# A decode layer bound by its loads: V in 32 KB runs over four large slots, P turned by selection products, wo in one transfer

## The chip, the cores and the metric

One core of a Trainium2 chip. The metric is the device time of one execution in microseconds. The kernel before takes 214.79 us (median of 3 runs, 214.47 to 214.87). Faster or slower needs 2%, here 4.3 us; each step is timed in five rounds against the kernel before on the same chip.

## The reference, cut to what matters

```python
x = layernorm(A_x)                                 # 4 batches, 1 token, D = 576
q = (x @ wq)                                       # 32 heads of 128
k, v = k_cache[:, :, -2048:], v_cache[:, :, -2048:]  # 16 heads, each for two q heads; 33.5 MB each
p = softmax(q k^T * 128**-0.5)
attn = (p v) @ wo                                  # wo: 4096 x 576, 4.7 MB
h  = gelu(layernorm(x) @ w1); x1 = x + shifted(h) @ w2
mlp  = x1 + gelu(layernorm(x1) @ w3) @ w4          # w3, w4: 5.3 MB each
out = A_x + attn + mlp
```

Everything is bf16 and almost everything is read once: 88.5 MB for four tokens.

## The kernel before

A single queue of transfers runs from the first microsecond to the last: weights, 16 chunks of K, 16 chunks of V with half of wo between them, the other half of wo, w4 in five pieces. The MLP is computed at the start, only its product with w4 waits for the end. The parts that the change touches:

```python
# four slots of 2 MB for K and then for V; chunk c is 4 heads of one batch, 16 KB runs
def kv_pairs(cache, c):
    b, gq = CH[c]
    return [(ring_t[:, (c % NPOS) * UE:(c % NPOS + 1) * UE],
             cache[b, NU * gq:NU * gq + NU, Sk - W:Sk, :].rearrange("g (i t) d -> i g (t d)", t=NT))]
...
for c in range(NC):
    add_dma(kv_pairs(A_v_cache, c), ("v", c % NPOS), [f"PV{c - NPOS}" if c >= NPOS else t_done(c + NC - NPOS)], KS + c)
# wo in two halves: one behind the fourth V chunk, one behind the last (WO_AT = (3.5, 15.5))
ev_wo = [add_dma([(wo_v[:, 16 * h:16 * h + 16, :], wo_s[:, 16 * h:16 * h + 16, :])], ("wo", h), ["h2_3"], KS + WO_AT[h]) for h in range(2)]
...
# P turned: transpose on DVE, one product with a permutation, copy on ACT
add("dve", lambda e, q=q: e.transpose(out=PTx[:, q, :], in_=P_sb[:, q, :]), waits=[f"exp{q}"], ...)
...
# product with V: 64 matmuls of N = 8 a chunk
ins = e.matmul(o_, lhsT=slot_t(c)[:, t, :], rhs=PTpad[:, c % 2, t].rearrange("p u e -> p (u e)"), ...)
...
# product with wo: 32 matmuls for each half, each half waiting for its own transfer
for h in range(2):
    add("pe", pe_AO(h), waits=["ORT", ev_wo[h]], sig=f"AO{h}", key=KT - 1 + 0.1 * h)
...
IDLE = ((3, -2.7), (7, 0.5), (5, 20.5))   # matmuls on zeros near the end, to hold PE's clock up
```

## Time and profile before

| | kernel before |
|---|---|
| time, span of the profiled run | 214.79 us, 213.3 us |
| read | 88.5 MB, 415 GB/s over the span |
| transfer engines in the V stage | full, 428 GB/s |
| PE in the V stage | 11.09 us busy of 30, at half clock |
| last links of the chain | w4's transfer, then 1.4 us of PE and a copy |

PE is the matmul engine (TensorE), DVE is VectorE, ACT is ScalarE, Pool is GpSimd; DMA stands for the 16 transfer engines. A "run" of V, K or wo is one piece of memory without a gap, moved by one transfer record; "clock" is the share of its full clock that PE was granted.

The views are read from the whole to the part: the page's forty slices tell which engine is full when, the chain tells what ended last, the windows give a stage's busy times, and the timeline gives durations and, in square brackets, how long an engine stood idle before an entry and for whom. The lines are shown in the prediction.

### The profile page before, as it was taken

Reading aid. Unit: us, or ns where it says so; the run is one execution under the profiler, and the core shown is the slowest. Engines: PE = TensorE matmul, PEld = TensorE weight load, DVE = VectorE, ACT = ScalarE, POOL = GpSimd, SP = SyncE. Lnnn points to the kernel's source line nnn. Section 1 sums busy time; section 2 is a strip of 40 time slices with the busy share of each in tenths; the row PEclk is TensorE's granted clock in tenths of the full one; section 3 lists DMA queues with packets and bytes.
Section 4 is the critical chain, followed back from the end, with each engine's and each line's share of the span. In section 5 each row is a group of like instructions: output and inputs, shape, how many; then the busy total and the mean of one; then the engine's idle time right before and its main releaser. Section 6 shows DMA issues by size and latency. Waiting matters only on the chain. (4 is left out here: it accounts for less than half of the span.)

```text
span 213.3 us, 5930 instructions
## 1 busy us (share of the span) xinstructions
PE 143.1 (67%) x2679; PEld 110.1 (52%) x2679; DVE 75.3 (35%) x148; ACT 61.6 (29%) x76; POOL 10.9 (5%) x38
## 2 busy tenths in 40 slices
PE   0048469999999999999996377133434433336995
PEld 0023246887788878888774067133434433334542
DVE  0242700767666666666664830100010001001000
ACT  2001204566556666666656620000000000000000
POOL 8300000000010000000000000000000000000000
PEclk9999959999999999999999555555555555555799
DMA  7999999999999999999999999999999999999993
GB/s 289 413 389 480 422 406 427 424 429 424 430 427 427 433 427 427 426 430 430 424 433 427 421 440 417 421 433 427 424 424 433 427 424 433 430 426 437 426 405 131
DMA packets 6446, 88.65 MB, mean 416 GB/s; under 512 B 744, under 2 KB 884, under 8 KB 1444
## 3 DMA queue, kind: packets, MB, share of 16 engines
q1 hardware_dynamic: 6420, 88.50, 97.8%
q8 instruction: 8, 0.13, 0.2%
q14 instruction: 2, 0.02, 0.0%
q10 hardware_dynamic: 16, 0.01, 0.0%
HBM read 88.49 MB, written 0.00 MB: 415 GB/s over the span
## 5 line engine op out<-in xcount | busy, mean ns | idle before, releaser
L343 PE MATMUL ps<-perm_bf,ring 128*128 128x128 bf16 x1024 | 62.1, 219 | 0.9
L343 PEld LDWEIGHTS ps<-perm_bf,ring 128*128 128x128 bf16 x1024 | 57.5, 98 | 9.6 <-issue 9.4
L350 DVE COPY kt<-ps 128x1024 bf16<-128x1024 bf16 x80 | 52.3, 687 | 26.1 <-PE ps L343 25.9
L349 ACT ACTIVATE kt<-ps 128x1024 bf16<-128x1024 bf16 x48 | 48.9, 1025 | 30.1 <-PE ps L343 28.9
L424 PE MATMUL ps<-PTpad,ring 128*128 128x8 bf16 x1024 | 29.7, 168 | 41.3 <-PEq L586 37.6
L424 PEld LDWEIGHTS ps<-PTpad,ring 128*128 128x128 bf16 x1024 | 28.7, 104 | 42.5 <-issue 42.4
L563 ACT ACTIVATE out_sb<-ps 4x288 bf16<-4x288 f32 x1 | 0.4, 403 | 87.4 <-PE ps L441 87.4
L357 PE MATMUL ps<-kt,Qs 128*32 128x512 bf16 x272 | 17.8, 382 | 1.4 <-PEq L586 1.4
L413 DVE TENSOR_TENSOR PTpad<-PT,mU_bf 128x512 bf16<-128x512 bf16 x16 | 6.4, 422 | 30.1 <-PE ps L424 30.1
L436 DVE TENSOR_TENSOR OTn<-ps,rinvB 128x32 bf16<-128x32 f32 x4 | 0.8, 192 | 33.9 <-PE ps L424 33.9
L279 PE MATMUL ps<-ident_bf,xn_bf 4*128 4x4 bf16 x8 | 0.6, 170 | 13.7 <-DVE ragsrc L273 13.7
L357 PEld LDWEIGHTS ps<-kt,Qs 128*32 128x32 bf16 x272 | 5.7, 95 | 6.8 <-issue 1.5
L378 POOL COPY Qs<-Qpad 128x128 bf16<-128x128 bf16 x16 | 4.6, 296 | 86.4 <-PE ps L357 72.4
L279 PEld LDWEIGHTS ps<-ident_bf,xn_bf 4*128 4x128 bf16 x8 | 0.4, 112 | 13.7 <-issue 11.3
L525 PE MATMUL ps<-w,x1nT 128*32 128x387 bf16 (+7 forms) x90 | 6.0, 411 | 2.1 <-DMA w<-in_B_w_dram 1.8
L525 PEld LDWEIGHTS ps<-w,x1nT 128*32 128x32 bf16 x90 | 4.6, 126 | 3.4 <-DMA w<-in_B_w_dram 2.1
L441 PE MATMUL ps<-w,ORT 128*4 128x288 bf16 x64 | 5.5, 344 | 0.4 <-DVE ORT L463 0.4
L562 DVE CAST out_sb<-ps 4x288 bf16<-4x288 f32 x1 | 0.4, 445 | 14.5 <-PE ps L441 14.5
L441 PE MATMUL ps<-w,h2T_sb 128*4 128x288 bf16 x72 | 5.0, 286 | 0.6 <-DMA w<-in_B_w_dram 0.6
L395 PE MATMUL ps<-kt,permT_bf 128*128 128x512 bf16 x4 | 2.4, 608 | 4.3 <-DVE kt L394 4.1
L263 ACT ACTIVATE sd<-mv 4x1 f32<-4x1 f32 x3 | 0.6, 203 | 14.5 <-DVE mv L261 14.5
L441 PEld LDWEIGHTS ps<-w,ORT 128*4 128x4 bf16 x64 | 3.2, 102 | 2.9 <-DVE ORT L463 1.0
(102 smaller groups left out, 65.7 us busy)
## 6 DMA issues: line engine op xcount, KB each, us to landing
ring<-in_A_k_cache_dram SPq DMA_DIRECT2D x16, 2048.0 KB, 14.4
ring<-in_A_v_cache_dram SPq DMA_DIRECT2D x16, 2048.0 KB, 17.4
w<-in_B_w_dram SPq DMA_DIRECT2D x1, 4608.0 KB, 24.1
w<-in_A_wo_dram SPq DMA_DIRECT2D x2, 2304.0 KB, 21.0
kt<-in_A_wq_dram SPq DMA_DIRECT2D x1, 4096.0 KB, 13.2
w<-in_B_w_dram SPq DMA_DIRECT2D x1, 2592.0 KB, 28.0
w<-in_B_w_dram SPq DMA_DIRECT2D x3, 576.0 KB, 14.2
w<-in_B_w_dram SPq DMA_DIRECT2D x1, 1296.0 KB, 30.6
```

Of the source, the lines that this page charges most:

```text
L279: e.transpose(XTps[idx][:, r, :], v[:, r, :], ident_bf[0:B, 0:B])
L343: ins = e.transpose(tb[n % 4][:, t, :], slot_t(c)[:, 8 * k + t, :], perm_bf[:])
L349: return "act", lambda e: e.activation(out=ktbuf[:, n % 16], in_=tb[n % 4], func=ACTF.Copy)
L350: return "dve", lambda e: e.tensor_copy(out=ktbuf[:, n % 16], in_=tb[n % 4])
L357: ins = e.matmul(Sps[32 * u:32 * u + 32, q, :].rearrange("p (t i) -> p t i", t=16), lhsT=Qs[:, c % NPOS, 32 * u:32 * u + 32], rhs=ktgrp[:, ...
L378: P(lambda e, c=c, cc=cc: e.tensor_copy(out=Qs[:, c % NPOS, :], in_=Qpad_t[:, 128 * cc:128 * cc + 128]), waits=["qT", "qs_zero"] + ([f"SC{ ...
L395: add("pe", lambda e, q=q: e.matmul(ps[:, 4 + q % 3, :], lhsT=permT_bf[:], rhs=PTx[:, q, :], start=True, stop=True), waits=[f"PTx{q}", "pe ...
L413: return lambda e: e.tensor_tensor(out=PTpad[:, c % 2], in0=PTv[:, :, cc, :].unsqueeze(2).to_broadcast([128, NT, NU, 2]), in1=mU_bf[:].uns ...
L424: ins = e.matmul(o_, lhsT=slot_t(c)[:, t, :], rhs=PTpad[:, c % 2, t].rearrange("p u e -> p (u e)"), start=(t == 0), stop=(t == NT - 1))
L436: add("dve", lambda e, hv=hv: e.tensor_tensor(out=hv(OTn), in0=OTps.rearrange("p (b h) -> p b h", b=B), in1=hv(rinvB), op=ALU.mult), waits ...
L441: return e.matmul(ACC[h], lhsT=lhsT, rhs=rhs, start=start, stop=stop, tile_position=(0, 32 * h), skip_group_check=True)
L525: ins = e.matmul(H2ps[k][32 * g:32 * g + 32, :].rearrange("p (x c) -> p x c", c=9)[:, :, off:off + cnt], lhsT=x_, rhs=w[:, base_:base_ + 1 ...
```

## The change

The intent is to carry V in half as many runs of twice the length. A transfer is now 4 MB: the 32 heads of two batches, a quarter of the keys, so each partition gets a run of 32 KB. Four slots of 4 MB are found in the rooms of w4, w3 and the ring. Since heads now lie across the partitions, P has to be turned otherwise: the exponentials are written with a stride, and 16 products with 0/1 selection matrices bring the right rows together. The product with V has N = 64 instead of 8, its operand is made by DVE in quarters ("pads"). wo moves into a V slot, so it can only come behind V, and comes whole.

```diff
-WO_AT = (3.5, 15.5)
-HOPS = (("K", 15), ("V", 2))
+HOPS = (("K", 15), ("V", 5))
...
+        vslot = [w4_t[:, 0:VE], w3_t[:, 0:VE], ring_t[:, 0:VE], ring_t[:, VE:2 * VE]]
+        P_exp = P_sb.rearrange("p (i q t) -> p q t i", i=NI, q=4)
...
-        for c in range(NC):
-            add_dma(kv_pairs(A_v_cache, c), ("v", c % NPOS), [f"PV{c - NPOS}" if c >= NPOS else t_done(c + NC - NPOS)], KS + c)
-        ev_wo = [add_dma([(wo_v[:, 16 * h:16 * h + 16, :], wo_s[:, 16 * h:16 * h + 16, :])], ("wo", h), ["h2_3"], KS + WO_AT[h]) for h in range(2)]
+        for c in range(8):
+            b, q = c // 4, c % 4
+            add_dma([(vslot[q], v_heads[32 * b:32 * b + 32, Sk - W + 4 * VT * q:Sk - W + 4 * VT * (q + 1), :].rearrange("h (i t) d -> h i (t d)", i=4))],
+                    ("v", q), [f"PV{c - 4}_3"] if b else v_free[q], KS + c)
+        ev_wo = add_dma([(w4_t[:, 0:32 * D], A_wo.rearrange("(p r) n -> p (r n)", r=32))], "wo", ["PV4_3"], KS + 8)
...
-            add("dve", lambda e, q=q: e.transpose(out=PTx[:, q, :], in_=P_sb[:, q, :]), waits=[f"exp{q}"], sig=f"PTx{q}", key=k0)
+                for i in range(4):
+                    ins = e.matmul(ps[:, 4 + g, :].rearrange("p (q t) -> p q t", q=4), lhsT=sel[:, g // 2, g % 2, i, :], rhs=P_v[:, i],
+                                   start=(i == 0), stop=(i == 3))
...
-                    ins = e.matmul(o_, lhsT=slot_t(c)[:, t, :], rhs=PTpad[:, c % 2, t].rearrange("p u e -> p (u e)"),
+                for t in range(VQ):
+                    ins = e.matmul(OTps, lhsT=vt[:, VQ * j + t, :], rhs=pads[:, j, t].rearrange("p h e -> p (h e)"),
...
-        for h in range(2):
-            add("pe", pe_AO(h), waits=["ORT", ev_wo[h]], sig=f"AO{h}", key=KT - 1 + 0.1 * h)
+        add("pe", pe_AO, waits=["ORT", ev_wo], sig="AO", key=KT - 1)
```

More of the change, by code (lines that the diff above doesn't have):

```diff
@@ L70, in bass_parallel_sum__sliding_block_cached__mixer_s_mlp__decode_kernel @@
         w4_t = sb("w4", [128, 36 * D], BF16)
-        PTpad_t = sb("PTpad", [128, 2 * NT * 2 * NU], BF16)
+        sel_t = sb("sel", [128, 16 * 128], BF16)
         PT_t = sb("PT", [128, NT * 32], BF16)
@@ L75, in bass_parallel_sum__sliding_block_cached__mixer_s_mlp__decode_kernel @@
         ktgrp = kt_t[:].rearrange("p (s t u i) -> p s t u i", s=8, t=16, u=NU)
-        P_sb = kt_t[:, 0:2048].rearrange("p (q x) -> p q x", q=4)
-        PTx = kt_t[:, 2048:4096].rearrange("p (q x) -> p q x", q=4)
-        PTpad = PTpad_t[:].rearrange("p (s t u e) -> p s t u e", s=2, t=NT, u=NU)
-        PTv = PT_t[:].rearrange("p (t c e) -> p t c e", t=NT, c=NC)
+        VT = W // 16
+        VE = VT * Dh
+        VQ = VT // 4
+        vslot = [w4_t[:, 0:VE], w3_t[:, 0:VE], ring_t[:, 0:VE], ring_t[:, VE:2 * VE]]
+        P_sb = kt_t[:, 0:W]
+        P_exp = P_sb.rearrange("p (i q t) -> p q t i", i=NI, q=4)
+        P_v = P_sb.rearrange("p (q i t) -> p i q t", q=4, i=4)
+        pads = kt_t[:, 2 * W:2 * W + 4 * VQ * 64].rearrange("p (j t h e) -> p j t h e", j=4, t=VQ, e=2)
+        PTv = PT_t[:].rearrange("p (b q t e) -> p b q t e", b=2, q=4, e=2)
+        sel = sel_t[:].rearrange("p (b e i x) -> p b e i x", b=2, e=2, i=4)
         wqmain = kt_t[:].rearrange("p (r n) -> p r n", r=4)
-        q_sb = PTpad_t[:, 0:1024]
+        q_sb = sel_t[:, 0:1024]
         h2g = PT_t[:, 0:1152]
-        wo_v = w3_t[:, 0:32 * D].rearrange("p (r n) -> p r n", r=32)
+        wo_v = w4_t[:, 0:32 * D].rearrange("p (r n) -> p r n", r=32)
         w3r = [w3_t[:, r * F:(r + 1) * F] for r in range(4)]
@@ L116, in bass_parallel_sum__sliding_block_cached__mixer_s_mlp__decode_kernel @@
         ones_f = sb("ones_f", [128, 128], FP32)
-        mU = sb("mU", [128, NU], FP32)
-        mU_bf = sb("mU_bf", [128, NU, 2], BF16)
+        mU = sb("mU", [128, 32], FP32)
+        mU_bf = sb("mU_bf", [128, 32, 2], BF16)
         diag = sb("diag", [128, 128], FP32)
@@ L138, in bass_parallel_sum__sliding_block_cached__mixer_s_mlp__decode_kernel @@
         rinvps = ps[:, 3, 0:128]
-        OTps = ps[:, 6, 0:32]
+        OTps = ps[:, 2, 256:320]
         Qps = [ps[:, 4 + k, :] for k in range(2)]
@@ L208, in bass_parallel_sum__sliding_block_cached__mixer_s_mlp__decode_kernel @@
         P(lambda e: e.memset(ones_f[:], 1.0), sig="ones_f", key=-89)
-        add("dve", lambda e: e.tensor_reduce(out=mU[:], in_=ident_f[:].rearrange("p (i u) -> p u i", u=NU), axis=AX.X, op=ALU.add),
+        add("dve", lambda e: e.tensor_reduce(out=mU[:], in_=ident_f[:].rearrange("p (h i) -> p h i", i=4), axis=AX.X, op=ALU.add),
             waits=["ident_f"], sig="mU", key=-8)
+        P(lambda e: e.memset(sel_t[:], 0.0), waits=["qTp"], sig="sel_zero", key=3.5)
+        ident_s = ident_bf[:].rearrange("p (u b x e) -> p b e x u", u=NU, b=2, x=8)
+        for n in range(16):
+            b, e_, i = n // 8, n // 4 % 2, n % 4
+            P(lambda e, b=b, e_=e_, i=i: e.tensor_copy(out=sel[:, b, e_, i, :].rearrange("p (x u k) -> p x u k", u=NU, k=4)[..., i], in_=ident_s[:, b, e_]),
+              waits=["sel_zero", "ident_bf"], sig=f"sel{n}", key=3.51 + 0.01 * n)
         for x in range(2):
@@ L233, in bass_parallel_sum__sliding_block_cached__mixer_s_mlp__decode_kernel @@
             add_dma(kv_pairs(A_k_cache, c), ("k", c % NPOS), [t_done(c - NPOS)] if c >= NPOS else [], c)
-        for c in range(NC):
-            add_dma(kv_pairs(A_v_cache, c), ("v", c % NPOS), [f"PV{c - NPOS}" if c >= NPOS else t_done(c + NC - NPOS)], KS + c)
-        wo_s = A_wo.rearrange("(p r) n -> p r n", r=32)
-        ev_wo = [add_dma([(wo_v[:, 16 * h:16 * h + 16, :], wo_s[:, 16 * h:16 * h + 16, :])], ("wo", h), ["h2_3"], KS + WO_AT[h]) for h in range(2)]
+        v_heads = A_v_cache.rearrange("b h s d -> (b h) s d")
+        v_free = [["hT1", "hs1", "h2_3"], ["h2_3"], [t_done(NC - 3)], [t_done(NC - 1)]]
+        for c in range(8):
[3 more added lines that the diff above has]
+        ev_wo = add_dma([(w4_t[:, 0:32 * D], A_wo.rearrange("(p r) n -> p (r n)", r=32))], "wo", ["PV4_3"], KS + 8)
         w4tile, w4cols, ev_w4, W4N = [], [], [], []
@@ L240, in bass_parallel_sum__sliding_block_cached__mixer_s_mlp__decode_kernel @@
         for n, rc in enumerate(W4_ROWS):
-            v = w4_t[:, len(w4tile) * D:(len(w4tile) + rc) * D]
+            t0 = len(w4tile)
+            v = w3_t[:, t0 * D:(t0 + rc) * D] if n < 2 else ring_t[:, (t0 - 27) * D:(t0 - 27 + rc) * D]
             ev_w4.append(add_dma([(v, B_w4[base:base + 128 * rc, :].rearrange("(p r) n -> p (r n)", r=rc))], ("w4", n),
-                                 ["hT1", "hs1", "h2_3"] if n == 0 else [], KT + 5 + n))
-            W4N.append((len(w4tile), len(w4tile) + rc))
+                                 ["PV5_3" if n < 2 else "PV6_3"], KT + 5 + n))
+            W4N.append((t0, t0 + rc))
             for r in range(rc):
@@ L387, in bass_parallel_sum__sliding_block_cached__mixer_s_mlp__decode_kernel, with pe_PT, f @@
         for q in range(4):
-            add("act", lambda e, q=q: e.activation(out=P_sb[:, q, :], in_=Sps[:, q, :], func=ACTF.Exp,
+            add("act", lambda e, q=q: e.activation(out=P_exp[:, q], in_=Sps[:, q, :].rearrange("p (t i) -> p t i", t=16), func=ACTF.Exp,
                                                    bias=negb[:, 0:1], scale=scale, accum_out=rs4[:, q:q + 1]),
                 waits=["negb"], sig=f"exp{q}", key=KS + 0.1 + 0.01 * q)
-        for q in range(4):
-            k0 = KS + 0.2 + 0.1 * q
-            add("dve", lambda e, q=q: e.transpose(out=PTx[:, q, :], in_=P_sb[:, q, :]), waits=[f"exp{q}"], sig=f"PTx{q}", key=k0)
-            add("pe", lambda e, q=q: e.matmul(ps[:, 4 + q % 3, :], lhsT=permT_bf[:], rhs=PTx[:, q, :], start=True, stop=True),
-                waits=[f"PTx{q}", "permT_bf"] + (["PT0"] if q == 3 else []), sig=f"PTy{q}", key=k0)
-            add("act", lambda e, q=q: e.activation(out=PT_t[:, 512 * q:512 * (q + 1)], in_=ps[:, 4 + q % 3, :], func=ACTF.Copy),
-                waits=[f"PTy{q}"], sig=f"PT{q}", key=k0 + 0.16)
+        def pe_PT(g):
+            def f(e):
+                ins = None
+                for i in range(4):
+                    ins = e.matmul(ps[:, 4 + g, :].rearrange("p (q t) -> p q t", q=4), lhsT=sel[:, g // 2, g % 2, i, :], rhs=P_v[:, i],
+                                   start=(i == 0), stop=(i == 3))
+                return ins
+            return f
+        for g in range(4):
+            add("pe", pe_PT(g), waits=[f"exp{q}" for q in range(4)] + ["sel15"], sig=f"PTy{g}", key=KS + 0.2 + 0.1 * g)
+            pt_o = PTv[:, g // 2, :, :, g % 2]
+            pt_i = ps[:, 4 + g, :].rearrange("p (q t) -> p q t", q=4)
+            if g % 2 == 0:
+                add("act", lambda e, o=pt_o, i=pt_i: e.activation(out=o, in_=i, func=ACTF.Copy), waits=[f"PTy{g}"], sig=f"PT{g}", key=KS + 0.3 + 0.1 * g)
+            else:
+                add("dve", lambda e, o=pt_o, i=pt_i: e.tensor_copy(out=o, in_=i), waits=[f"PTy{g}"], sig=f"PT{g}", key=KS + 0.9 + 2 * (g // 2))
         add("dve", lambda e: e.tensor_reduce(out=rsum[:], in_=rs4[:], axis=AX.X, op=ALU.add), waits=["exp3"], sig="rsum", key=KS + 0.8)
@@ L403, in bass_parallel_sum__sliding_block_cached__mixer_s_mlp__decode_kernel @@
         add("pe", lambda e: e.matmul(rinvps, lhsT=ones_f[:], rhs=diag[:], start=True, stop=True), waits=["diag", "ones_f", "exp3"],
-            sig="rinvp", key=KS + 0.9)
+            sig="rinvp", key=KS + 0.55)
         add("dve", lambda e: e.tensor_copy(out=rinvB[:].rearrange("p (c u e) -> p c u e", u=NU, e=2),
                                            in_=rinvps.rearrange("p (u c e) -> p c u e", u=NU, e=2)),
-            waits=["rinvp"], sig="rinvB", key=KS + 1.5)
-        def dve_pad(c):
-            b, gq = CH[c]
-            cc = 4 * b + gq
-            return lambda e: e.tensor_tensor(out=PTpad[:, c % 2],
-                                             in0=PTv[:, :, cc, :].unsqueeze(2).to_broadcast([128, NT, NU, 2]),
-                                             in1=mU_bf[:].unsqueeze(1).to_broadcast([128, NT, NU, 2]), op=ALU.mult)
@@ L417, in pe_PV, with dve_pad @@
-        def pe_PV(c):
-            b, gq = CH[c]
-            o_ = OTps[:, 8 * b:8 * b + 8]
+            waits=["rinvp"], sig="rinvB", key=KS + 2)
+        def dve_pad(c, j):
+            b, q = c // 4, c % 4
+            return lambda e: e.tensor_tensor(out=pads[:, j],
+                                             in0=PTv[:, b, q, VQ * j:VQ * (j + 1), :].unsqueeze(2).to_broadcast([128, VQ, 32, 2]),
+                                             in1=mU_bf[:].unsqueeze(1).to_broadcast([128, VQ, 32, 2]), op=ALU.mult)
@@ L421, in f, with pe_PV @@
+        def pe_PV(c, j):
+            q = c % 4
+            vt = vslot[q].rearrange("p (t d) -> p t d", t=VT)
             def f(e):
                 ins = None
-                for t in range(NT):
-                    ins = e.matmul(o_, lhsT=slot_t(c)[:, t, :], rhs=PTpad[:, c % 2, t].rearrange("p u e -> p (u e)"),
-                                   start=(t == 0), stop=(t == NT - 1))
-                return ins
-            return f
-        for c in range(NC):
-            w = [f"PV{c - 2}"] if c >= 2 else [f"PT{q}" for q in range(4)] + ["mU_bf1"]
-            b, gq = CH[c]
-            add("dve", dve_pad(c), waits=w, inc=[(tok("pad"), 1)], key=KV + 2 * max(c - 1, 0) + 0.2)
-            add("pe", pe_PV(c), waits=[take("pad"), take(("v", c % NPOS), 16)] + ([take("otn")] if b == 0 else []), sig=f"PV{c}",
-                key=KV + 2 * c, loop=("V", gq))
-            if b == B - 1:
-                hv = lambda t, gq=gq: t[:, 0:128].rearrange("p (b h) -> p b h", b=B)[:, :, 8 * gq:8 * gq + 8]
-                add("dve", lambda e, hv=hv: e.tensor_tensor(out=hv(OTn), in0=OTps.rearrange("p (b h) -> p b h", b=B), in1=hv(rinvB), op=ALU.mult),
-                    waits=["rinvB", f"PV{c}"], sig=f"OTn{gq}" if gq == 3 else None, inc=[(tok("otn"), 1)] if gq < 3 else [], key=KV + 2 * c + 0.1)
@@ new lines, in f @@
+                for t in range(VQ):
+                    ins = e.matmul(OTps, lhsT=vt[:, VQ * j + t, :], rhs=pads[:, j, t].rearrange("p h e -> p (h e)"),
+                                   start=(q == 0 and j == 0 and t == 0), stop=(q == 3 and j == 3 and t == VQ - 1))
+                return ins
+            return f
+        for c in range(8):
+            b, q = c // 4, c % 4
+            for j in range(4):
+                add("dve", dve_pad(c, j), waits=[f"PV{c - 1}_{j}"] if c else [f"PT{g}" for g in ((0, 1) if j == 0 else (2, 3))] + ["mU_bf1"],
+                    inc=[(tok("pad"), 1)], key=KV + 2 * c + 0.2 * j)
+                add("pe", pe_PV(c, j), waits=[take("pad")] + ([take(("v", q), 16)] if j == 0 else []) + ([take("otn")] if j == 0 and q == 0 else []),
+                    sig=f"PV{c}_{j}", key=KV + 2 * c + 0.2 * j, loop=("V", b))
+            if q == 3:
+                cols = slice(64 * b, 64 * b + 64)
+                add("dve", lambda e, cols=cols: e.tensor_tensor(out=OTn[:, cols], in0=OTps, in1=rinvB[:, cols], op=ALU.mult),
+                    waits=["rinvB", f"PV{c}_3"], sig="OTn1" if b else None, inc=[] if b else [(tok("otn"), 1)], key=KV + 2 * c + 2.5)
@@ L449, in pe_idle, with pe_AO @@
             return f
-        def pe_AO(half):
-            def f(e):
-                ins = None
-                for r in range(16 * half, 16 * half + 16):
-                    for h in range(2):
-                        ins = acc_mm(e, h, ORT[:, :, r], wo_v[:, r, HALF * h:HALF * (h + 1)], start=(r == 0))
-                return ins
-            return f
+        def pe_AO(e):
+            ins = None
+            for r in range(32):
+                for h in range(2):
+                    ins = acc_mm(e, h, ORT[:, :, r], wo_v[:, r, HALF * h:HALF * (h + 1)], start=(r == 0))
+            return ins
         KH = -58.0
-        add("dve", lambda e: e.transpose(out=OTy[:].rearrange("p b r -> p (b r)"), in_=OTn[:]), waits=["OTn3"], sig="OTy", key=KT - 3)
+        add("dve", lambda e: e.transpose(out=OTy[:].rearrange("p b r -> p (b r)"), in_=OTn[:]), waits=["OTn1"], sig="OTy", key=KT - 3)
         add("pe", lambda e: e.matmul(ORps, lhsT=permT_bf[:], rhs=OTy[:].rearrange("p b r -> p (b r)"), start=True, stop=True),
@@ L463, in bass_parallel_sum__sliding_block_cached__mixer_s_mlp__decode_kernel @@
         add("dve", lambda e: e.tensor_copy(out=ORT[:].rearrange("p b r -> p (b r)"), in_=ORps), waits=["ORp"], sig="ORT", key=KT - 2)
-        for h in range(2):
-            add("pe", pe_AO(h), waits=["ORT", ev_wo[h]], sig=f"AO{h}", key=KT - 1 + 0.1 * h)
+        add("pe", pe_AO, waits=["ORT", ev_wo], sig="AO", key=KT - 1)
         def pe_t1(e):
```

## The prediction

> **What bounds the kernel now.** I read the page's slices first, because they tell which engine is full at every moment, then the chain that ended last, then the windows by stage, then the order of time in the V stage and at the end. The three lines of the page on transfers:
>
> ```profile
> DMA  7999999999999999999999999999999999999993
> GB/s 289 413 389 480 422 406 427 424 429 424 430 427 427 433 427 427 426 430 430 424 433 427 421 440 417 421 433 427 424 424 433 427 424 433 430 426 437 426 405 131
> DMA packets 6446, 88.65 MB, mean 416 GB/s; under 512 B 744, under 2 KB 884, under 8 KB 1444
> ```
>
> The transfer engines are full in every slice but the first and the last, at about 427 GB/s, whatever the compute engines do. The kernel reads 88.65 MB and the change reads the same bytes. The windows by stage (length, then busy time of each engine, then clock, DMA share, GB/s) say the same for K and for V:
>
> ```profile
> 45.00:105.00 60.00, 59.22 (x991) 48.66 (x989) 40.52 (x62) 38.13 (x38) 3.26 (x11) 1.00 1.01 428
> 142.00:172.00 30.00, 11.09 (x384) 10.74 (x384) 2.14 (x6) 0.00 (x0) 0.00 (x0) 0.50 1.01 428
> ```
>
> In the V stage PE works 11.09 of 30 us, and at half clock; DVE works 2.14. What V waits for is the landing of V. The chain in order of time ends so:
>
> ```profile
> 177.79 32.21 DMA w<-in_B_w_dram
> 210.00 0.04 issue
> 210.04 1.40 PE ps L441 x18
> 211.44 0.43 DVE out_sb L562
> ```
>
> The last link is the queue of transfers itself; PE adds a tail of some 1.4 us and one copy. So a change is worth what it takes off the transfers' total, unless it empties the queue on the way or lengthens what PE has to do after the last landings. The timeline around the last V chunks shows the pitch of a transfer:
>
> ```profile
> 183.54 1.85 PE L424 MATMUL ps<-PTpad,ring 128*128 128x8 bf16 x64 [2.90 <-PEq L586]
> 188.43 1.85 PE L424 MATMUL ps<-PTpad,ring 128*128 128x8 bf16 x64 [3.04 <-PEq L586]
> 193.32 1.85 PE L424 MATMUL ps<-PTpad,ring 128*128 128x8 bf16 x64 [3.04 <-PEq L586]
> ```
>
> One 2 MB chunk (128 runs of 16 KB) each 4.89 us. With 128 runs over 16 engines each engine carries 8 runs, so 611 ns a run; the single transfer records of the trace have a median of 613 ns for a 16 KB run.
>
> **What the Trainium skill says.** (1) "DMA: Bandwidth & Descriptors", section "Why small descriptors are slow (HBM only)": a fixed cost per packet and per descriptor comes on top of the bytes; its section on 436 GB/s puts a ceiling of 435.2 GB/s on the ports. The trace agrees in kind: the records' medians are 613 ns for 16 KB, 688 for 18 KB, 773 for 20.25 KB, 1213 for 32 KB (wq) and 1364 for 36 KB (w3). From 16 to 32 KB the slope is 600 ns for 16 KB more, so 13 ns of each run are fixed: 427.6 GB/s at 16 KB and 432 at 32 KB. (2) Same page, "Latency and other measured facts", the row on HBM row pitch at large powers of two: copies with a row pitch of 512 KiB ran at 207 GB/s per direction, 2 MiB at 164, 4 MiB at 103, a padded pitch at 214. (3) Same page, "The descriptor swizzle": each engine writes four neighbouring partitions of each half. Before, four neighbouring partitions are the same 16 KB piece of four heads, so the engines read 16 KB apart inside one head; after, they are the four 32 KB pieces of one head, so the engines read one head (8192 keys x 128 x 2 B = 2 MiB) apart. The page's pitch of 512 KiB puts its engines also four rows, 2 MiB, apart, and lost 3% (207 against 214). No run here shows yet what this does to loads. (4) "TensorE: Matmul & The Clock Gate", "Wait — 56ns, not 53.3ns?": back to back, a matmul takes N / 1.2 GHz at half clock and never less than about 25 ns. The trace has 64 matmuls of N=8 in 1.85 us, 29 ns each, which agrees with a floor.
>
> **The change part by part.**
> V's runs. Before: 16 chunks x 8 runs per engine = 128 runs x 613 ns = 78.46 us. After: 8 x 8 = 64 runs x 1213 ns = 77.63 us. Gain 0.83 us, on the path that sets the end.
> wo whole. Before 2 x 8 runs of 18 KB x 688 ns = 11.01 us; after 8 runs of 36 KB x 1364 ns = 10.91. Gain 0.10 us, on the path. w4 keeps its five pieces. Sum of the queue: -0.93 us.
> Product with V. Still 1024 matmuls, but N goes from 8 to 64. At half clock that is an estimate of 64/1.2 = 53 ns, so 128 x 53 = 6.8 us for each 4 MB chunk; at full clock the 29 ns floor gives 3.7. A chunk lands every 8 x 1213 ns = 9.7 us, so it stays hidden.
> Pads on DVE. Before 422 ns for 512 columns, 16 times. After 2048 columns, 32 times: at most 4 x 422 = 1.69 us, 6.8 us per chunk. They wait only for the preceding product on the same quarter, so they are made while V is still in flight: hidden.
> The turn of P. Removed: four DVE transposes (2.7 us) and four products. Added: 16 selection products of N=512, at half clock 512/1.2 = 427 ns each, 6.8 us, after all four exponentials. Before, exp ended at 121.95 and the first product started at 125.29; after, I put it at 122 + 6.8 + 0.8 (last copy) + 1.7 (pad) = about 131. The first chunk's slot is free at about 138.
> Does the queue run dry? The last V landing before is at 193.3 with 16 x 4.89 + 5.5 (half of wo) behind K, so K ended near 109.6. Four slots of 9.7 us reach to 148.4; the fifth transfer needs the first slot, free at 138: 10 us to spare. Later each slot frees some 7 us after its landing with 29 us queued. wo needs chunk 4 used, w4 chunks 5 and 6: each is issued before the transfer ahead of it is through. Never dry.
> The selection matrices: one clearing (Pool's Qpad clearing of 2080 columns took 1.82 us) and 16 small copies, early in the K stage, when Pool has over 70 us of idle: nothing.
> The end on PE. Before, half of wo was there at 196.97 and the first half of that product ran early. After, whole wo lands where its second half did, 193.3 + 5.5 - 0.93 = 197.9. The 64 matmuls took 5.48 us, partly at half clock; w4's products took 36 in 2.37 us, 66 ns each, so 4.2 to 5.5 us. With the small product 0.65, warming 1.69, w4's parts 2.37 + 1.25 + 1.27 and the last 18 in 1.3, PE ends between 210.5 (limited by the transfers) and 211.9, against 211.4 before. So between nothing and 1.4 us of the queue's gain can be taken back here; I charge 0.25.
> Total: 214.79 - 0.93 + 0.25 = 214.1 us.
>
> **The rivals.**
> A. The transfers slow down because the 16 engines read at 2 MiB multiples in step. For: the skill's row; the transfers before are laid out so that engines are 16 KB apart. Against: at that spacing the page lost only 3%, and within each engine 128 KB are read in one piece. 3% of 77.63 is 2.4 us: 216.5. If the loss were that of the 2 MiB row (164 of 214), V would take 101 us and the kernel 238.
> B. The tail: PE, not the last transfer, sets the end, since no part of wo's product can run early. It makes 214.3 to 215.2.
> C. PE or DVE becomes the bound of the V stage. For: at half clock PE is busy 6.8 of 9.7 us, and DVE up to 6.8. Against: both have about 30% to spare, a PE that busy might be granted its full clock, and four slots absorb jitter. If both ran in series, 13.6 us per chunk, it would add some 31 us; the quarters, each with its own pad, are there to prevent that.
> D. Nothing: run length does not matter, and 613 against half of 1213 is noise of different places in the kernel: 214.8.
>
> **Range and chances.** The plain sum is -0.4%. A gain over 2% would need 4.3 us, but at the ports' ceiling of 435.2 all 88.65 MB would take 203.7 us and V itself could win only 78.46 - 77.1 = 1.4 us; so 1%. A loss over 2% needs 4.3 us more, that is A worse than the comparable row of the skill, or C: 11%. The rest, 88%, is within 2%. Predicted 214.1 us; range 213.3 to 217.0, the upper side long because of A.
>
> **What would show it.** Right: GB/s of some 431 in the V slices, landings of V about 9.7 us apart, DMA at 9 in all slices, still a chain that ends in w4's transfer. Product with V of about 53 ns per matmul at half clock, or 29 at full. Wrong by A: V slices under 420 GB/s with the DMA share still 1.00. Wrong by B: a chain whose last 10 us are PE, with wo's product starting near 198 and no wait for w4's last piece. Wrong by C: DMA tenths under 9 in the V stage and the queue waiting for PE's products just before it issues.

## The result, and the profile after

The changed kernel takes 216.43 us (median of 6 runs, 215.72 to 217.06), the kernel before 214.59 in the same rounds. The ratio is 1.0082 (95% interval 1.0057 to 1.0107). A ratio is the mean time of one kernel's runs over that of the other's of the same rounds, so not quite the ratio of the medians quoted. Executions over 1.5% slower than the fastest of the same kernel are left out of the means. So the kernel is 0.8% slower: within 2%, and inside the predicted range, but on the other side of zero from the predicted 214.1. Note also the scatter: 1.3 us from run to run where the kernel before has 0.4. The profiled run is the slowest of the six (217.06, span 215.7).

The slices of the changed kernel (clock of PE in tenths, share of the transfer engines, GB/s):

```profile
PEclk9999969999999999999999556999799967888599
DMA  7999999999999999999999999999999999999970
GB/s 292 402 404 462 437 407 425 422 427 422 428 434 425 422 434 425 433 428 425 441 431 444 431 437 428 425 434 422 437 416 444 413 456 413 447 410 429 405 317 5
```

The queue never runs dry in the V stage, as predicted, but it is over before the span is: the last slice has 5 GB/s where the kernel before had 131. The window of the V stage, in the changed kernel:

```profile
142.00:172.00 30.00, 21.11 (x629) 20.31 (x625) 24.60 (x23) 0.00 (x0) 0.00 (x0) 0.94 1.01 431
```

V moves at 431 GB/s instead of 428. PE and DVE are far busier than before (21.11 and 24.60 of 30 us against 11.09 and 2.14) and still have room. The chain that ended last, in order of time:

```profile
165.09 34.05 DMA w<-in_A_wo_dram
199.13 0.14 issue
199.27 7.16 PE ps L465 x68
206.43 0.16 issue
206.59 1.46 PE ps L471 x6
208.04 2.30 PE ps L465 x36
210.34 1.18 PE ps L471 x5
211.53 2.35 PE ps L465 x36
213.87 0.43 DVE out_sb L583
```

It ends no longer with w4's transfer but with wo's, and behind it stand 14.6 us of PE without a wait for data: the products with wo and w4 (L465) and the matmuls on zeros (L471). The timelines of PE's end, first the kernel before:

```profile
196.97 5.48 PE L441 MATMUL ps<-w,ORT 128*4 128x288 bf16 x64 [0.38 <-DVE ORT L463]
202.37 0.65 PE L441 MATMUL ps<-t,ident_f 4*4 4x288 f32 x4
202.96 1.69 PE L447 MATMUL ps<-zeros_bf 128*128 128x512 bf16 x7
204.91 2.37 PE L441 MATMUL ps<-w,h2T_sb 128*4 128x288 bf16 x36 [0.26 <-DMA w<-in_B_w_dram]
```

and the changed kernel:

```profile
193.15 0.23 PE L483 MATMUL ps<-OTy,permT_bf 128*128 128x128 bf16 x1
199.27 6.58 PE L465 MATMUL ps<-w,ORT 128*4 128x288 bf16 x64 [5.89 <-DMA w<-in_A_wo_dram]
205.78 0.65 PE L465 MATMUL ps<-t,ident_f 4*4 4x288 f32 x4
207.97 2.37 PE L465 MATMUL ps<-w,h2T_sb 128*4 128x288 bf16 x36
```

Before, the product with wo began at 196.97, when its operand was ready. After, PE stands still for 5.89 us until wo has landed at 199.27 and then needs 6.58 us for the same 64 matmuls. Before, PE had to wait 0.26 us for w4 at 204.91; after, w4's pieces lie ready at 207.97. So two things are to be explained: why PE's end grew, and why wo landed at 199.27 when the sum had it at 197.9.

Inside the turn of P one term was far from its estimate without harm. The exponentials, before and after:

```profile
L388 ACT ACTIVATE kt<-ps,negb 128x512 bf16<-128x512 f32 x4 | 2.7, 686 | 2.6 <-DVE negb L385 2.6
```

```profile
L403 ACT ACTIVATE kt<-ps,negb 128x512 bf16<-128x512 f32 x4 | 9.4, 2702 | 2.6 <-DVE negb L400 2.6
```

Written with a stride of 64 elements, the same 512 results take 2702 ns instead of 686. The first product with V starts at 137.2 instead of the estimated 131. The slots cover it: the next transfer of V was issued at 141.3, about 7 us before the queue would have been empty (estimated at 148.4 in the prediction).

**The theories.** T, "tail": PE's work behind the landing of wo sets the end, and it is long because the clock falls to half while PE waits. Its rivals: R, "transfers": the last landing itself is later, PE only happens to end there; W, "work": the 64 matmuls need 6.6 us at any clock; and for what remains, F, "fetch": PE's instruction fetches, which run on the same transfer engines, hold up one of them.

### The profile page after: what moved, and what is told of

Same layout as the page of the kernel before. It is cut to its first block, busy times and chain, and to the rows that moved or that the text cites. A ratio compares the mean times of both kernels' runs of the same rounds, so it can differ in the third digit from the quotient of the medians.

```text
span 215.7 us, 5968 instructions
## 1 busy us (share of the span) xinstructions
PE 153.5 (71%) x2688; PEld 118.5 (55%) x2691; DVE 104.4 (48%) x160; ACT 67.9 (31%) x74; POOL 15.5 (7%) x55
## 5 line engine op out<-in xcount | busy, mean ns | idle before, releaser
L364 ACT ACTIVATE kt<-ps 128x1024 bf16<-128x1024 bf16 x48 | 49.1, 1024 | 31.1 <-PE ps L358 29.8
L436 DVE TENSOR_TENSOR kt<-PT,mU_bf 128x2048 bf16<-128x2048 bf16 x32 | 37.1, 1217 | 10.3 <-PE ps L447 10.1
L447 PE MATMUL ps<-kt,ring 128*128 128x64 bf16 x512 | 20.2, 211 | 14.5 <-PEq L607 10.2
L447 PEld LDWEIGHTS ps<-kt,ring 128*128 128x128 bf16 x512 | 19.7, 110 | 14.9 <-issue 14.9
L447 PE MATMUL ps<-kt,w 128*128 128x64 bf16 x512 | 16.3, 193 | 7.0 <-PEq L607 5.8
L447 PEld LDWEIGHTS ps<-kt,w 128*128 128x128 bf16 x512 | 15.5, 98 | 7.8 <-issue 7.4
L411 PE MATMUL ps<-kt,sel 128*128 128x512 bf16 x16 | 5.5, 516 | 12.2 <-ACT kt L403 12.2
L465 PE MATMUL ps<-w,ORT 128*4 128x288 bf16 x64 | 6.6, 392 | 5.9 <-DMA w<-in_A_wo_dram 5.9
L411 PEld LDWEIGHTS ps<-kt,sel 128*128 128x128 bf16 x16 | 1.9, 124 | 15.8 <-ACT kt L403 12.7
L403 ACT ACTIVATE kt<-ps,negb 128x512 bf16<-128x512 f32 x4 | 9.4, 2702 | 2.6 <-DVE negb L400 2.6
L465 PEld LDWEIGHTS ps<-w,ORT 128*4 128x4 bf16 x64 | 3.9, 115 | 8.4 <-issue 6.0
```

What stands on the lines that cost most here:

```text
L364: return "act", lambda e: e.activation(out=ktbuf[:, n % 16], in_=tb[n % 4], func=ACTF.Copy)
L403: add("act", lambda e, q=q: e.activation(out=P_exp[:, q], in_=Sps[:, q, :].rearrange("p (t i) -> p t i", t=16), func=ACTF.Exp, bias=negb[: ...
L411: ins = e.matmul(ps[:, 4 + g, :].rearrange("p (q t) -> p q t", q=4), lhsT=sel[:, g // 2, g % 2, i, :], rhs=P_v[:, i], start=(i == 0), stop ...
L436: return lambda e: e.tensor_tensor(out=pads[:, j], in0=PTv[:, b, q, VQ * j:VQ * (j + 1), :].unsqueeze(2).to_broadcast([128, VQ, 32, 2]), i ...
L447: ins = e.matmul(OTps, lhsT=vt[:, VQ * j + t, :], rhs=pads[:, j, t].rearrange("p h e -> p (h e)"), start=(q == 0 and j == 0 and t == 0), s ...
L465: return e.matmul(ACC[h], lhsT=lhsT, rhs=rhs, start=start, stop=stop, tile_position=(0, 32 * h), skip_group_check=True)
```

## The experiments

Unless said otherwise a run has five rounds. Times are medians.

**e1: wo in halves again, behind V.**

```diff
-        ev_wo = add_dma([(w4_t[:, 0:32 * D], A_wo....)], "wo", ["PV4_3"], KS + 8)
+        ev_wo = [add_dma([(w4_t[:, 16 * h * D:16 * (h + 1) * D], wo_s[:, 16 * h * D:16 * (h + 1) * D])], ("wo", h), ["PV4_3"], KS + 8 + 0.1 * h)
+                 for h in range(2)]
-        add("pe", pe_AO, waits=["ORT", ev_wo], sig="AO", key=KT - 1)
+        for h in range(2):
+            add("pe", pe_AO(h), waits=["ORT", ev_wo[h]], sig=f"AO{h}", key=KT - 1 + 0.1 * h)
```

> The changed kernel, but wo comes in two transfers of 2.36 MB again, one behind the other after V, and its 64 products with wo in two groups of 32, each waiting for its own half. Theory 'tail' (PE's work behind the landing of wo sets the end): the first 32 products run before wo's second half lands, PE has some 3 us less to do behind it, PE waits for the last piece of w4 again, and the time falls from 216.4 to about 215 (limited by the last landing, which in the changed kernel's profile was some 0.6 us later than before). Rival 'transfers' (the last landing sets the end): no change, or 0.1 us more for the shorter runs: 216.4.

Measured: 215.33 us (215.0 to 216.92), ratio 1.0045 (1.0018 to 1.0071). PE's timeline:

```profile
193.65 2.13 PE L467 MATMUL ps<-w,ORT 128*4 128x288 bf16 x32 [0.38 <-DVE ORT L489]
199.34 3.15 PE L467 MATMUL ps<-w,ORT 128*4 128x288 bf16 x32 [3.57 <-DMA w<-in_A_wo_dram]
```

The first half now runs at 193.65 and 1.1 us of the loss is gone; R alone is out. But in this profile the second half, still behind an idle stretch, takes 3.15 us where the first took 2.13, and the rest of PE's end was again without waits. Half the work moved, the clock not cured.

**e2: PE kept busy until wo lands.**

```diff
-IDLE = ((3, -2.7), (7, 0.5), (5, 20.5))
+IDLE = ((3, -2.7), (20, -1.5), (7, 0.5), (5, 20.5))
```

> The changed kernel, but 20 matmuls on zeros are put on PE between the turn of the output and the product with wo, so that PE has no idle stretch before wo lands. Theory 'clock' (the 64 products with wo ran 6.58 us because the clock had fallen to half in the 5.9 us in which PE waited): they take 4.2 us now, and the time falls by up to 2.4 us, to about 214.5 to 215.2, with less scatter from run to run. Rival 'work' (the 64 products take 6.6 us whatever the clock): time unchanged at 216.4 or later by up to 0.5. Rival 'transfers': unchanged.

Measured: 215.19 us (215.03 to 215.21), ratio 1.0028 (1.0015 to 1.0041), against 216.43 for the changed kernel. PE's timeline:

```profile
194.00 4.48 PE L471 MATMUL ps<-zeros_bf 128*128 128x512 bf16 x20
199.20 4.09 PE L465 MATMUL ps<-w,ORT 128*4 128x288 bf16 x64 [0.72 <-DMA w<-in_A_wo_dram]
```

Twenty matmuls on zeros fill the gap, and the same 64 products take 4.09 us instead of 6.58, with wo landing at the same moment. That refutes W. The clock in the same stretches, the changed kernel and then e2:

```profile
197.00:199.00 2.00, 0.00 (x0) 0.00 (x0) 0.00 (x0) 0.00 (x0) 0.00 (x0) 0.64 0.97 415
199.00:201.00 2.00, 1.73 (x16) 1.05 (x18) 0.00 (x0) 0.00 (x0) 0.00 (x0) 0.50 1.02 435
```

```profile
197.00:199.00 2.00, 1.48 (x7) 0.49 (x5) 0.00 (x0) 0.00 (x0) 0.00 (x0) 1.00 1.02 435
199.00:201.00 2.00, 1.80 (x30) 1.48 (x32) 0.00 (x0) 0.00 (x0) 0.00 (x0) 1.00 0.99 425
```

So the clock did fall inside the gap, and did not where the gap was filled. The scatter falls from 1.3 us to 0.2, so nearly all of it came with PE's end. The chain ends with w4's transfer again. T is shown, and its size: 216.43 - 215.19 = 1.24 us.

**b1: the kernel before, with wo alone moved.**

```diff
-        ev_wo = [add_dma([(wo_v[:, 16 * h:16 * h + 16, :], ...)], ("wo", h), ["h2_3"], KS + WO_AT[h]) for h in range(2)]
+        ev_wo = add_dma([(w3_t[:, 0:32 * D], A_wo.rearrange("(p r) n -> p (r n)", r=32))], "wo", ["h2_3"], KS + 15.5)
```

(and the 64 products in one group, as in the change)

> The kernel before with one part of the change alone: wo in one transfer behind all of V, and its 64 products in one group. Theory 'tail': nothing is gained or lost in the bytes, but PE waits for wo at half clock and has all 64 products to do behind its landing (198.8): time 216 to 217, with PE at the end of the chain and no wait for w4's last piece. Rival (the tail is peculiar to the new V stage): unchanged at 214.5.

Measured: 218.29 us (217.63 to 219.05), ratio 1.0183 (1.0167 to 1.0199): more than expected, 3.8 us for this one part. PE's timeline:

```profile
200.83 5.53 PE L441 MATMUL ps<-w,ORT 128*4 128x288 bf16 x64 [7.66 <-DMA w<-in_A_wo_dram]
```

Here PE waits 7.66 us, and from wo's landing to the last copy it works 13.6 us without a wait for data (14.6 in the changed kernel). So the tail does not belong to the new V stage, it belongs to wo coming late and whole. But b1 is no clean test of its size, because the edit did a second thing. The half of wo that stood between the fourth and the fifth V chunk had kept the queue filled while P was turned; without it the queue runs short, as the window shows (the kernel before, then b1):

```profile
125.00:130.00 5.00, 3.48 (x125) 3.45 (x126) 0.61 (x2) 0.00 (x0) 0.00 (x0) 0.50 1.02 428
125.00:130.00 5.00, 4.53 (x161) 4.48 (x162) 1.15 (x3) 0.00 (x0) 0.00 (x0) 0.50 0.71 265
```

By the transfer records, counted as below from the mean end of w3, the last piece of w4 lands 2.1 us later than in the kernel before. The profiled run of b1 is 3.0 us over that of the kernel before, so about 0.9 us are left for PE's tail (an estimate from one profile each).

**e3: V in 16 KB runs, all else as changed.**

```diff
-            add_dma([(vslot[q], v_heads[...].rearrange("h (i t) d -> h i (t d)", i=4))],
+            add_dma([(vslot[q][:, VE // 2 * x:VE // 2 * (x + 1)], v_src[:, :, VE // 2 * x:VE // 2 * (x + 1)]) for x in range(2)],
-                ... [take(("v", q), 16)] ...
+                ... [take(("v", q), 32)] ...
```

> The changed kernel with V in runs of 16 KB: each 4 MB chunk is two transfers of 2 MB (each takes half of every 32 KB run), all else as it is. By the sum of the prediction V costs 128 x 613 against 64 x 1213 ns for each transfer engine, 0.83 us more: the landing of the last V chunk and of wo come 0.8 us later and the time goes to about 217.2, with V slices of 428 instead of 432 GB/s. Rival (run length does nothing, 432 is an accident of the place): unchanged at 216.4 and 432 GB/s.

Measured: 217.5 us (216.29 to 218.18), ratio 1.0138 (1.0110 to 1.0166). About 1.1 us more than the changed kernel, in the expected direction; but with PE's tail at the end the scatter is as large as the effect. The window of the V stage has 426 GB/s. Hence:

**e5: the same on top of e2**, where the last landing sets the end.

> The kernel e2_pe_warm (PE kept busy ahead of wo, so that the last landing sets the end: 215.19) with V in runs of 16 KB as in e3. Only the run length differs from e2, and the tail of PE no longer adds its scatter. By the prediction's term (128 x 613 against 64 x 1213 ns): 0.83 us more, 216.0. Rival (the longer runs gain nothing at the last landing, since the slowest transfer engine sets it): 215.2.

Measured: 215.94 us (215.45 to 216.12), ratio 1.0059 (1.0045 to 1.0073), so 0.75 us more than e2 with its 32 KB runs. The windows of the V stage, e2 and then e5:

```profile
142.00:172.00 30.00, 23.08 (x680) 22.58 (x677) 24.75 (x24) 0.00 (x0) 0.00 (x0) 0.89 1.01 430
```

```profile
142.00:172.00 30.00, 22.52 (x690) 21.94 (x686) 25.04 (x24) 0.00 (x0) 0.00 (x0) 0.94 1.01 425
```

The term for the run length, 0.83 us, is right within the scatter. So the change does gain what it was made for. Yet e2, which has this gain and no tail, is still 0.6 us behind the kernel before (ratio 1.0028). About 1.4 us are lost elsewhere at the last landing.

**Where the rest goes: the slowest of 16 engines.** A transfer has landed when all 16 transfer engines have done their eight runs, so the landing is that of the latest engine, while GB/s is their mean. The single transfer records make this visible: at each change of size (V to wo, wo to w4) the first record of the new size is found for each of the 16 engines. The records carry no number of their engine; each is put behind the record that ends where it begins, and such a reconstruction is good to some 0.06 us. The result, in us; "lag" is how far the latest engine is behind the mean of the 16, in the one profiled run, while the time is the median of all runs:

| kernel | instruction fetches in all | lag at the end of V | lag at the end of wo | time |
|---|---|---|---|---|
| before | 8 | 0.97 | 0.97 | 214.5 |
| b1 | 8 | 1.35 | 1.36 | 218.29 |
| changed | 10 | 0.72 | 1.97 | 216.43 |
| e1 | 10 | 0.75 | 1.95 | 215.33 |
| e2 | 10 | 1.41 | 1.76 | 215.19 |
| e3 | 10 | 0.71 | 1.91 | 217.5 |
| e5 | 10 | 0.78 | 1.94 | 215.94 |
| e4 (below) | 14 | 1.75 | 1.62 | 217.06 |

Counted from the mean end of w3, where both kernels still do the same, the mean engine reaches w4's first piece after 169.67 us before and after 169.17 us in the changed kernel: 0.50 us earlier. The latest engine reaches it after 170.64 and 171.14: 0.50 us later. The gain is there on average and gone at the latest engine, which in the changed kernel falls back by 1.25 us while wo is moving. At that moment, about 1 us before the mean engine is through with wo, the records show one 16 KB fetch of instructions, 1.10 us long, and the run of wo that begins where it ends took 1.83 us instead of 1.36. The other fetches of the changed kernel's V stage look alike: 1.06 to 1.10 us, and behind each a run of V about 0.5 us longer than the median of 1.216. Fetch and longer run together take about 1.55 us of one engine. Followed from record to record, the engine with the fetch in wo is the latest one at w4's first piece, in the changed kernel and also in e1, e2, e3, e5, e6 and e7. In the changed kernel the second latest engine is 0.62 us behind the mean, so without this one fetch wo would have landed some 1.3 us earlier (an estimate: 1.97 - 0.62). The kernel before has no fetch between its V stage and the last pieces of w4. The queue of such fetches, in the kernel before, the changed kernel and e4:

```profile
q8 instruction: 8, 0.13, 0.2%
```

```profile
q8 instruction: 10, 0.16, 0.3%
```

```profile
q8 instruction: 14, 0.23, 0.4%
```

This is theory F: the new loop over V is twice as long in instructions (1024 matmuls' worth of two instructions in 2 passes instead of 4), so more of them have to be fetched, by the engines that carry the data. That the fetch delays the latest engine is read from the records; that the longer loop is what puts a fetch there is so far argued.

**e4: the loop over V written out straight**, so PE has twice the instructions for V. With the loop goes the branch inside it.

```diff
-HOPS = (("K", 15), ("V", 5))
+HOPS = (("K", 15),)
...
-                    sig=f"PV{c}_{j}", key=KV + 2 * c + 0.2 * j, loop=("V", b))
+                    sig=f"PV{c}_{j}", key=KV + 2 * c + 0.2 * j)
```

> The changed kernel with PE's loop over V written out straight: twice the PE instructions for V, none executed more often. The changed kernel's trace shows 10 instruction fetches of 16 KB of about 1.05 us each, before shows 8, and the transfers' spread over the 16 engines is larger (w4's first piece took 9.7 us from its first packet to its last, before 8.4, where 6.2 would do). Theory 'fetches' (each instruction fetch delays the one transfer engine it runs on, and the slowest engine sets every landing): some 4 fetches more, spread up by 0.5 to 2 us, last landings later, time 216.5 to 218. Rival: no more spread, time 216.4.

Measured: 217.06 us (215.14 to 217.36), ratio 1.0103 (1.0072 to 1.0134), not to be told from the changed kernel's 1.0082. There are four fetches more, as expected, all in the V stage; there the mean engine comes 0.40 us later (16 x 0.40 / 4 = 1.6 us of one engine for each fetch; set against e2, whose mean engine is 0.18 us later than the changed kernel's, it is 0.9) and the lag at the end of V grows from 0.72 to 1.75. But the fetch during wo then hit another engine than the latest, and the lag at the end of wo is 1.62 against 1.97. So fetches cost engine time, that is shown, and the size agrees with the 1.55 us of the records; more of them did not make the last landing later, as the theory in its simple form had it. It matters whom they hit.

**e6 and e7: the branch in the loop over V left out, or moved** (put there, it seems, to steer the fetching; no run shows why), on top of e2.

```diff
-HOPS = (("K", 15), ("V", 5))
+HOPS = (("K", 15),)                # e6
+HOPS = (("K", 15), ("V", 11))      # e7
```

> The kernel e2_pe_warm without the branch inside PE's loop over V. Nothing of the data changes, only when PE fetches its instructions and so which transfer engine is held up when. Theory 'fetches' (who carries the instruction fetches decides how late the slowest engine is): the last landing moves by some 0.4 to 1.2 us in one direction, time between 214.2 and 216.4. Rival (the slowest engine is slow for another reason, such as the layout of V): time 215.2, same spread of the engines' ends.

> The kernel e2_pe_warm with the branch inside PE's loop over V after the twelfth product instead of the sixth. As for e6: by 'fetches' the last landing moves by 0.4 to 1.2 us in one direction; by the rival it stays and the time is 215.2.

Measured: 215.13 us (214.98 to 215.43), ratio 1.0029 (1.0015 to 1.0043), and 215.16 us (214.96 to 215.2), ratio 1.0026 (1.0012 to 1.0039). No change in time. But they did not test what they should: both still have 10 fetches, one of them about 1 and 2 us before the mean engine ends wo, and the lag again grows during wo, from 0.83 to 2.05 and from 0.74 to 2.07. As tests of the time they neither speak for F nor refute it; in both the latest engine is again the one with that fetch.

**Three shifts of PE's code**, by 64, 128 and 192 instructions ahead of the K stage, on top of e2 (n = 32, 64, 96).

```diff
+        def pe_shift(e):
+            for _ in range(n):
+                ins = e.matmul(ps[:, 4, 0:8], lhsT=zeros_bf[:, 0:128], rhs=zeros_bf[:, 0:8], start=True, stop=True)
+            return ins
+        add("pe", pe_shift, waits=["zeros_bf"], sig=None, key=-0.45)
```

> The kernel e2_pe_warm with 32 matmuls of N=8 on zeros (64 PE instructions, about 1 us) ahead of the K stage, so that all later PE code stands 64 instructions further on. In the traces of all kernels with the new V stage but e4 one transfer engine loses about 1.3 us while wo is on its way, at the moment of a 16 KB instruction fetch, and it is then the slowest one up to the end; before has no fetch there. Theory 'fetch': with the code at another place the fetch comes at another time or hits another engine; where no fetch falls on one of the late engines the last landing comes up to 1.2 us earlier, and the time is 214.0 to 214.4 instead of 215.2. Rival (the slowest engine is slow in wo whatever PE's code): 215.2.

> As s_shift_64 with 64 such matmuls (128 instructions, about 2 us). By 'fetch' at least one of the three shifts moves the time to 214.0 to 214.4; by the rival all three stay at 215.2.

> As s_shift_64 with 96 such matmuls (192 instructions, about 3 us). By 'fetch' at least one of the three shifts moves the time to 214.0 to 214.4; by the rival all three stay at 215.2.

Measured: 218.6 (ratio 1.0180, 1.0157 to 1.0202), 218.86 (1.0194, 1.0171 to 1.0217) and 219.38 us (1.0234, 1.0207 to 1.0261). All three miss both expectations, because the edit disturbed something else. PE's timeline of the first, at the start of the K stage:

```profile
35.67 0.94 PE L351 MATMUL ps<-zeros_bf 128*128 128x8 bf16 x32
42.54 3.57 PE L365 MATMUL ps<-perm_bf,ring 128*128 128x128 bf16 x32 [5.93 <-PEq L614]
```

PE stands still for 5.93 us in front of the K loop, held by its own sequencer, where e2 went on at once; the queue of K then runs short for a moment (its slices show 8 and 6 tenths). So the place of this code is worth over 3 us. That it was tuned by its author is a guess; that the standstill is a wait for instructions is not proven. For F the runs give a side result only: the fetch after V falls later there, within 0.5 us around the mean engine's end of wo, and the lag does not grow during wo (1.75 to 1.72, 1.73 to 1.66, 1.42 to 1.35).

**g: the same 64 instructions in the 12 us gap before the turn of P**, so that only the code of V and of the end moves, on top of e2.

> The kernel e2_pe_warm with 32 matmuls of N=8 on zeros between the last scores and the turn of P, where PE waits 12 us for the exponentials anyway. The code of the K stage stays where it was (the three shifts moved it and PE stood still for 4 to 6 us at the entry of the K loop), only the code of V and of the tail stands 64 instructions further on. Theory 'fetch': the instruction fetch that fell into wo's transfer in e2 comes at another time or hits another engine; if it hits none of the late engines the last landing comes up to 1.2 us earlier and the time is 214.0 to 214.8; if it hits one again, 215.2. Rival (one engine is slow in wo whatever PE's code): 215.2, with the latest engine again falling back by about 1.3 us during wo though no fetch lies there.

Measured: 215.22 us (215.08 to 215.25), ratio 1.0031 (1.0017 to 1.0044). There are 11 fetches; the one after V comes 0.4 us after the mean end of wo, and during wo the lag does not grow (2.07, then 2.0 to 2.07). So the rival, an engine that is slow in wo by nature, is refuted. But one engine was already 2.07 us late at the end of V, where this kernel has one fetch more (followed back, it had carried one of V's fetches), and the fetch after V then threw a second engine back, from about 0.6 to 1.85. Nothing is won.

| run | time, us | ratio to before | 95% interval |
|---|---|---|---|
| changed kernel | 216.43 | 1.0082 | 1.0057 to 1.0107 |
| e1 wo in halves | 215.33 | 1.0045 | 1.0018 to 1.0071 |
| e2 PE kept warm | 215.19 | 1.0028 | 1.0015 to 1.0041 |
| e5 e2 with 16 KB runs | 215.94 | 1.0059 | 1.0045 to 1.0073 |
| b1 before, wo last and whole | 218.29 | 1.0183 | 1.0167 to 1.0199 |

No version of the new V stage beat the kernel before. What weighs against F in its simple form is that the latest engine reaches w4's first piece 171.1 to 171.3 us after the mean end of w3 in the changed kernel, e1, e2, e4, e6, e7 and g alike, with 10, 11 or 14 fetches at different moments. What would have to be tried next is a shorter loop over V (two fetches fewer); with slots in three different tensors I had no such form.

## Why the prediction was right or wrong

The time lay in the range and the class (within 2%) was right, but the centre was 2.3 us low (214.1 against 216.43), and the sign was wrong. That the range held it is in part luck: its upper side was made long for rival A, which did not occur, while rival B, which did, had been put at 215.2 at most.

- **V's runs: right.** -0.83 us predicted; with the end set by the landing, 0.75 us measured (e5 against e2), and 431 GB/s in the V stage. The medians of V's own runs (614 and 1216 ns) give 0.77. This refutes rival D, that run length does nothing.
- **Queue never dry, product with V and pads hidden: right.** The transfer engines are full through V. A chunk's 128 products took 3.89 to 5.44 us, below the 6.8 estimated at half clock, because PE's clock went up and down between half and full; pads took 1217 ns, below the bound of 1690. Rival C did not occur.
- **The turn of P: mis-sized without effect.** The missed term is the exponential with its strided output, 2702 ns instead of 686.
- **Rival A, engines reading 2 MiB apart: refuted.** V was faster, 431 against 428 GB/s, though with longer runs. At the same run length too nothing was lost: the 16 KB runs of V have a median of 613 ns in e5, where the engines read 2 MiB apart, and 614 in the kernel before, where they read 16 KB apart.
- **The end on PE: the mechanism was right (it was rival B), the size wrong.** Charged with 0.25 us, it took 1.24 (e2). The prediction put the 64 products at 4.2 to 5.5 us; they took 6.58 in the profiled run, because it did not follow the clock through the idle stretch in front of them, which the change itself creates: V ends earlier in the queue than before, and wo lands no earlier.
- **"Sum of the queue: -0.93 us": the step that failed.** It was right for the mean of the engines in kind (0.50 us earlier at w4's first piece) and wrong for the one that counts. The latest engine comes 0.50 us later, and e2 is 0.6 us slower than before instead of 0.9 faster. The 1.5 us between them are the mis-sized term: about 0.4 in the mean engine, 0.2 of which two more fetches explain (2 x 1.55 / 16), and 1.0 in the lag of the latest, 1.97 against 0.97. The prediction multiplied runs by the duration of a run, as if all 16 engines kept step. One engine falls back by over a microsecond when a fetch of instructions is on the way. That a fetch takes about 1.55 us of one engine is shown (the records, and e4), that the engine so held up is the latest is read from the records, and that the fallback is not tied to wo is shown (g). That the longer loop is to blame for the whole of the 1.5 us is argued: no run had the new V stage with a lag as small as before's, so this part stays open.

The sum: e2 splits the measured +1.84 (216.43 - 214.59) into +1.24 from PE's end and +0.6 from the last landing; that the two add up is so by construction.

## What to carry to other kernels

When loads bound a kernel, add up the queue for the latest transfer engine, not for the mean: a gain of half a per cent in GB/s is easily lost to one engine that also carries something else, such as the instructions of a longer loop. Before moving a late operand still later, list what has to run behind its landing and at which clock: an engine that waits for it may come out of the wait slower than it went in. Here a one-line filler of matmuls on zeros gave back 1.24 us and nearly all the scatter.

## What the Trainium skill lacked or had wrong

- "DMA: Bandwidth & Descriptors", "Latency and other measured facts", the row on row pitch: it is measured on copies between memories and does not say what loads do. Here loads with the engines 2 MiB apart lost nothing: a 16 KB run took 613 ns (e5) against 614 with engines 16 KB apart (the kernel before).
- "Runtime: NRT & Kernel Launch", "Instruction fetch mechanics", has fetches in blocks of 16 KiB on a queue of their own and calls the cost of crossing a block mostly hidden. The runs agree on the size and show a cost that it lacks: a fetch record of 0.98 to 1.11 us (kernel before and changed kernel), and with the longer run behind it about 1.55 us of the time of one of the engines that carry the data (0.40 us in the mean of 16 for four fetches). No page that I read counts this in a load-bound kernel.
- The size of what a strided output costs on ScalarE. "SBUF — State Buffer" has a penalty for strides beyond a 16-byte line, without a number for this engine. Here 512 results took 2702 ns at a stride of 64 bf16 elements and 686 ns side by side.
